# Head 0's zero fills moved, two heads' loads gated later, and extra TensorE work at head ends, in a 32-head attention kernel

## The chip, the cores and the metric

The kernel runs on one core of a Trainium2 chip. A core has five engines that run side by side, each through its own list of instructions in order: TensorE (PE, matrix multiply, results to the memory PSUM), VectorE (DVE), ScalarE (ACT, exponentials), GpSimd (POOL) and SyncE (SP, which here does nothing but issue DMAs). They wait for each other through semaphores. The metric is the device time of the core in microseconds (us). The kernel before has a median of 642.9 us of 3 runs (640.63 to 644.48).

## The reference

```
eps = 1e-6                                  # q, k, v: 1 x 32 heads x 2048 x 20, t: 32, all bf16
qn = q / (jnp.sqrt((q * q).sum(axis=-1, keepdims=True)) + eps)
kn = k / (jnp.sqrt((k * k).sum(axis=-1, keepdims=True)) + eps)
logits = jnp.einsum('bhqd,bhkd->bhqk', qn, kn) * t[None, :, None, None]
attn = _softmax(logits, axis=-1)
return jnp.einsum('bhqk,bhkd->bhqd', attn, v)
```

It is attention with normed queries and keys and one factor t per head. The product of a query and a key is 20 long, so a head's work is not in the matrix products but in 2048 x 2048 exponentials, 134 million in all.

## The kernel before

**The flow of a head.** k and q of a head are loaded to `qk_sb` in five DMAs (one for k, four for q: `add_loads`, line 585), v in one to `vaug`. DVE squares and sums them (lines 650, 654), takes the inverse root by a few small steps (`rs_u` line 658 to `rs_r`), and norms (line 696). SP then issues a DMA transposition of the normed head to `qkT` (line 707), and, when that has landed, ten copies by DMA, the "rotations": four from `qkT` to `qz` and six to `kR` (lines 708 to 716). They lay queries and keys out so that TensorE can run a QK product, whose contraction is only 20 long and padded to 32 rows, in three ways: as "32 rows" (up to four products beside each other in the array), as "64 rows" or as "128 rows", with the moving operand taken from `qz`, whose other rows are zero. The result is the same; what differs is how much of the array works. For head 0 the way is shorter: TensorE transposes, six DVE copies turn the keys (`kx`, line 768, the last of them is `rot0`), and three DMA transpositions bring them to `kR`.

**Two ways to the exponential.** A head's keys make 16 row tiles. `DVE_TILES[h]` of them go to DVE, the rest to ACT. On ACT's side, units of 512 columns are put in waves of 2 and 3 PSUM banks in turn (`psA`, two slots); TensorE fills a wave (`qk_mm`, line 790), ACT takes one exponential over it (line 891) to `p_ring`. On DVE's side (`psD`, two banks), DVE turns the logits into 16-bit integers that, read as half floats, are an exponential in the rough (line 950, one instruction for two banks, or for one where the tile is in `SPLIT`), and three shifted copies of them (line 960 on DVE, or line 964 on POOL, in pieces that fit beside DVE's work) are added up with scaled v (`vph`) so that the errors cancel. The PV products (line 810) of both ways, four matmuls a group, one for each 32-column strip of the array, add up in one PSUM bank, `psO`. When a head's last PV group is in, DVE transposes `psO` (line 823); only then may the next head's first PV group write it. The transposed sums are divided and stored (lines 832, 840).

**The order of the work** is not written by hand. Each instruction is a `Task` with an estimated duration, dependencies and a priority, and `list_schedule` (line 114) plays the engines through in time: each engine takes, when it is free, the ready task that its rules prefer. A DMA task occupies SP for `dur` and lands `lat` later. What comes out is the order of each engine's list; the chip then runs the lists in order, each instruction behind its semaphore waits. So the estimates, the numbers in `KNOBS` and `STAGES` (one choice of rules for every 10 us of planned time) and the priorities set the order, and nothing else. A QK task has `modes`: the planner keeps a sum of the array work that TensorE did in the last `TICK` = 3.41 us and takes the wider form (mode 1) as long as that sum stays under `LOAD`.

**SP's list** holds all loads (but one), transpositions, rotations and stores. A load of head h (from head 3 on) waits for an earlier head's transposition, its gate: head 3 for head 0's, head 4 for head 1's, later heads for that of head h - 4 (line 588, "LGATE" is 0). The priorities put a transposition and rotations of a head before loads that are due later, but only among tasks that are ready; a load that is ready while a transposition is still on its way is issued first.

**Before the first head**, DVE and POOL fill buffers with zeros and ones. `qz[0]` is filled by DVE, `qz[1]` and `qz[2]` by four POOL memsets each (line 561): those of `qz[1]` as soon as POOL gets to them, those of `qz[2]` after `rot0`.

## Time and profile before

| what | us |
| --- | --- |
| median of 3 runs | 642.9 (640.63 to 644.48) |
| the profiled execution, its own time | 645.58 |
| span of the profiled execution, first to last instruction | 643.8 |
| mean granted TensorE clock, of full speed | 0.987 |
| first exponential of ACT starts | 9.26 |
| last exponential ends | 638.66 |

All durations below are from the profiled execution; the time around its span is 1.8 us. An engine's busy time counts instructions in execution. Matmuls are pipelined: a group of four shows 0.40 us from start to end, eight show 0.61. A line of the chain of waits names an engine and a line of the kernel; "SPq" is SP's queue, that is time in which DMAs were being issued. The granted clock is the share of full speed at which TensorE ran in that stretch. Line 511 is the helper of most fills, line 508 that of all plain DMAs, so those are told apart by what they write.

### The profile page before, as it was taken

The page shows a single profiled execution, that of the slowest core. Times are in us where ns is not written, and L with a number is a line of the kernel's source. Part 1 is how long each engine was busy: PE and PEld are TensorE (multiplying, and loading weights), DVE is VectorE, ACT ScalarE, POOL GpSimd, SP SyncE. Part 2 cuts the span into 40 slices and gives each one's busy share as a digit, 9 for nine tenths or more (in the row PEclk, how much of TensorE's full clock was granted, in tenths as well). Part 3 has the DMA queues.
Part 4 walks back from the last instruction along what each step waited for, and adds up shares of the span by engine and source line. Part 5 has one row for each costly group of instructions (what it writes and reads, how often), then busy time and mean ns, then how long its engine had stood idle before and what let it go on. Part 6 is the DMA issues. An engine that isn't in the chain of part 4 may idle for free.

```text
span 643.8 us, 15022 instructions
## 1 busy us (share of the span) xinstructions
PE 593.1 (92%) x6127; PEld 171.4 (27%) x6143; DVE 627.0 (97%) x920; ACT 626.9 (97%) x558; POOL 428.0 (66%) x460
## 2 busy tenths in 40 slices
PE   7887998799999989999999899999999999999997
PEld 2221222222222222222222222222222222222222
DVE  8997999999999999999999999999999999999997
ACT  6997999999999999999999999999999999999996
POOL 4154677468787776767777586776877377665653
PEclk9997999999999989999999899999999999999999
DMA  4554445244344414344243333333343242322000
GB/s 59 68 72 82 72 69 77 44 67 59 59 65 73 65 29 68 52 73 65 51 68 48 54 61 59 69 52 51 58 73 56 36 72 37 66 50 56 5 3 16
DMA packets 196916, 36.39 MB, mean 57 GB/s; under 512 B 172656, under 2 KB 196848, under 8 KB 196848
## 3 DMA queue, kind: packets, MB, share of 16 engines
q1 hardware_dynamic: 196656, 35.32, 34.5%
q8 instruction: 48, 0.79, 0.5%
q14 instruction: 20, 0.16, 0.1%
q10 hardware_dynamic: 192, 0.11, 0.1%
HBM read 7.87 MB, written 2.62 MB: 16 GB/s over the span
## 4 chain that ended last, share of the span: by engine, by line
ACT 61%; DVE 28%; PE 6%; SPq 2%; issue 2%; DMA 1%; DVEq 0%
ACT p_ring L891 61%; DVE xt L950 17%; DVE ss L960 5%; PE psO L810 2%; SPq L508 2%; PE psA L790 2%; PE psD L790 1%; DVE rs_sum L654 1%; DVE oT L823 1%; DVE qkn L696 1%; DVE sq L650 1%; DMA kR<-qkT 0%; DVE o_stage L840 0%; DVE rs_u L658 0%; DMA qz<-qkT 0%
## 5 line engine op out<-in xcount | busy, mean ns | idle before, releaser
L891 ACT ACTIVATE p_ring<-psA 128x1024 bf16<-128x1024 f32 (+1 forms) x551 | 623.3, 1451 | 6.8 <-PE psA L790 5.8
L964 POOL INT64_ADD ss<-xt x430 | 420.8, 982 | 201.6 <-DVE xt L950 67.8
L950 DVE TENSOR_SCALAR xt<-psD 128x1024 int16<-128x1024 f32 (+1 forms) x410 | 414.0, 1025 | 9.3 <-PE psD L790 7.8
L810 PE MATMUL psO<-ss,vph 128*32 128x512 f16 x2016 | 172.9, 387 | 0.0
L960 DVE TENSOR_SCALAR ss<-xt 128x2048 int16<-128x2048 int16 x178 | 121.5, 685 | 0.5
L790 PE MATMUL psA<-qkT,kR 32*128 32x512 bf16 x636 | 110.2, 388 | 11.3 <-ACT p_ring L891 10.8
L810 PE MATMUL psO<-p_ring,vaug 128*32 128x512 bf16 x1376 | 119.2, 388 | 0.0
L790 PE MATMUL psA<-qz,kR 64*128 64x512 bf16 (+1 forms) x389 | 100.7, 391 | 9.3 <-ACT p_ring L891 8.6
L790 PE MATMUL psD<-qz,kR 64*128 64x512 bf16 (+1 forms) x313 | 84.8, 389 | 3.9 <-DVE xt L950 2.6
L790 PE MATMUL psA<-qkT 32*128 32x512 bf16 x196 | 62.4, 386 | 4.7 <-ACT p_ring L891 4.3
L810 PE MATMUL psO<-xt,vaug 128*32 128x512 f16 x672 | 66.7, 387 | 0.0
L810 PEld LDWEIGHTS psO<-ss,vph 128*32 128x32 f16 x2016 | 44.4, 94 | 76.7 <-issue 65.1
L790 PE MATMUL psA<-qz,qkT 64*128 64x512 bf16 (+1 forms) x145 | 50.4, 390 | 4.6 <-ACT p_ring L891 4.4
L790 PE MATMUL psD<-qkT,kR 32*128 32x512 bf16 x186 | 48.9, 384 | 3.1 <-DVE xt L950 2.5
L790 PEld LDWEIGHTS psA<-qkT,kR 32*128 32x128 bf16 x636 | 26.5, 91 | 77.2 <-ACT p_ring L891 73.8
L810 PEld LDWEIGHTS psO<-p_ring,vaug 128*32 128x32 bf16 x1376 | 31.3, 94 | 57.4 <-issue 49.7
L790 PEld LDWEIGHTS psA<-qz,kR 64*128 64x128 bf16 (+1 forms) x396 | 24.2, 93 | 71.9 <-ACT p_ring L891 68.6
L790 PE MATMUL psD<-qz,qkT 64*128 64x512 bf16 (+1 forms) x102 | 38.8, 388 | 2.4 <-DMA qz<-qkT 1.3
L790 PEld LDWEIGHTS psD<-qz,kR 64*128 64x128 bf16 (+1 forms) x318 | 20.9, 93 | 46.0 <-DVE xt L950 40.0
L790 PE MATMUL psD<-qkT 32*128 32x512 bf16 x65 | 24.4, 386 | 4.9 <-DMA kR<-qkT 2.9
L810 PEld LDWEIGHTS psO<-xt,vaug 128*32 128x32 bf16 x672 | 17.5, 94 | 30.5 <-issue 24.7
L696 DVE TENSOR_TENSOR qkn<-qk_sb,rs_r 128x640 bf16<-128x640 bf16 x31 | 25.3, 816 | 0.0
(58 smaller groups left out, 199.5 us busy)
## 6 DMA issues: line engine op xcount, KB each, us to landing
kR<-qkT SPq DMA_DIRECT2D x62, 96.0 KB, 2.1
qz<-qkT SPq DMA_DIRECT2D x127, 32.0 KB, 1.8
kR<-qkT SPq DMA_DIRECT2D x62, 64.0 KB, 2.0
qk_sb<-in_k_dram SPq DMA_DIRECT2D x32, 80.0 KB, 2.8
vaug<-in_v_dram SPq DMA_DIRECT2D x32, 80.0 KB, 3.2
qk_sb<-in_q_dram SPq DMA_DIRECT2D x124, 20.0 KB, 2.5
out_dram<-o_stage SPq DMA_DIRECT2D x31, 80.0 KB, 1.8
kR<-qkT SPq DMA_DIRECT2D x62, 32.0 KB, 1.9
```

Of the source, the lines that this page charges most:

```text
L508: return add(eng, name, lambda e, tk: e.dma_start(dst, src), dur, deps, pri, lat=lat, dma=key)
L650: c = [dv("sq", lambda e, tk, x=x, y=src: e.tensor_tensor(y, x, x, ALU.mult), 0.065 + 0.3335 * m, [u for k in range(m) for u in lds[h + k] ...
L654: sums.append(dv("sum", lambda e, tk, i=i, k=k, src=src: e.tensor_reduce(rs["sum"][:, 2 * R * (i + k):2 * R * (i + k + 1)], src[:, 2 * R * ...
L696: norm[h] = [dv("norm", lambda e, tk, x=x, b=b, i=i: e.tensor_tensor(qkn[b][:, :, 0:D], x[:, :, :], bc(rs["r"][:, 2 * R * i:2 * R * (i + 1 ...
L790: return eng.matmul(dst, lhsT, mov, tile_position=(p0, 0))
L810: last = eng.matmul(psO[32 * g:32 * g + 32, :], w, rhs_of(g), start=start, stop=False, skip_group_check=True, tile_position=(0, 32 * g))
L823: trO[h] = add("DVE", f"tr{h}", lambda e, tk: e.transpose(oT_all[:, so, :, :].rearrange("p r d -> p (r d)"), psO[:, :]), 0.63, [lambda: pv ...
L891: act[w] = add("ACT", f"exp{w}", lambda e, tk: e.activation(p_ring[:, p0 * 512:p0 * 512 + n], psA[:, slot * WAVES[0] * 512:slot * WAVES[0] ...
L950: u = add("DVE", f"t1.{j}.{k0}", lambda e, tk, o=o, c=c, w=512 * m: e.tensor_scalar(xt[sx][:, o:o + w], psD[:, c:c + w], X_MUL, X_ADD, ALU ...
L960: f = add("DVE", f"s{i}.{js[0]}", lambda e, tk, i=i, dst=dst: e.tensor_scalar(dst[:, be:be + w], xt[0][:, bx:bx + w], float(PHASES[i]), No ...
L964: f.alt = lambda c, n, i=i, dst=dst: lambda e, tk: e.int64_add(dst[:, be + 2 * c:be + 2 * (c + n)].bitcast(I64), xt[0][:, bx + 2 * c:bx + ...
```

## The change

It has five parts.

1. The POOL fills of `qz[1]` wait for `rot0` too, as those of `qz[2]` did. A new small buffer `nil` is filled with zeros by POOL.
2. The gates of the loads come from a table for heads 3 to 6: head 3 waits for head 0's transposition, 4 for 1's, 5 for 2's, 6 for 3's; from head 7 on it stays head h - 4. Before, head 5 waited for 1's and head 6 for 2's. The planner's estimates for loads of k, q and v change.
3. A new rule, `fill`: where TensorE has nothing ready, the PV sum of the current head is still open, the next QK task is at least 0.15 us away and the work in the last 3.41 us is under 3700, it is given a group of four matmuls of `nil` (zero weights) with `ones`, added to `psO`.
4. While the sum is closed (the head's PV groups are all in, and the next head's have not begun), the choice between QK forms counts only the work that will still be within the 3.41 us 1.2 us later, and so takes the wide form more often, if ACT or DVE has time for it. Elsewhere `LOAD` falls from 3550 to 3400.
5. `STAGES` has other numbers, `SPLIT` loses tile 82 and gains 124 and 157, and `DVE_TILES` moves tiles: head 3 has 7 instead of 6, head 8 5 instead of 6, head 27 7 instead of 6, head 31 6 instead of 7.

```diff
-    LOAD = 3550.0
+    LOAD = 3400.0
...
+    FILL = 3700.0
+    AHEADL = 1.2
+    FGAP = 0.15
...
+        left = collections.Counter(t.head for t in self.tasks if t.head is not None)
+        bank = [None]
+        self.fillers = []
+
+        def fill(now):
+
+            if not self.filler or bank[0] is None or not left[bank[0]] or now < self.LIGHT:
+                return
+            then = min(list(soon["PE"].values()) + [now + 0.6])
+            if then - now < self.FGAP:
+                return
+            while recent and recent[0][0] < now - self.TICK:
+                recent.popleft()
+            if sum(w for e, w in recent if e > then - self.TICK) >= self.FILL:
+                return
+            t = self.filler()
...
+                if e == "PE" and free[e] <= now + 1e-9 and not ready[e]:
+                    fill(now)
...
-                    load = sum(w for _, w in recent)
-                    if load + t.work < self.LOAD:
+                    shut = bank[0] is not None and not left[bank[0]]
+                    load = sum(w for x, w in recent if not shut or x > now + self.AHEADL - self.TICK)
+                    slack = (free["ACT"] if t.name[2] == "A" else free["DVE"] + sum(r[2].dur for r in ready["DVE"])) - now - t.modes[1][2] - 0.5
+                    if load + t.work < self.LOAD and (not shut or slack > 0 or sum(w for _, w in recent) + t.work < self.LOAD):
...
+        nil = sbuf("nil", [128, 32], BF16)
...
+        z_nil = memset("POOL", nil[:, :], 0.0, 0.1, -71)
...
-                             [lambda: rot0] if i > 1 else [], -70 + i) for g in range(NG)])
+                             [lambda: rot0], -70 + i) for g in range(NG)])
...
-            war = (norm[h - NB] if h >= NB else []) + ([lambda: [trn[max(h - 3, 0) if h < 5 + LGATE else h - 4]]] if h >= EARLY else [lambda: q0] if h == 2 else [])
+            war = (norm[h - NB] if h >= NB else []) + ([lambda: [trn[{3: 0, 4: 1, 5: 2, 6: 3}.get(h, h - 4)]]] if h >= EARLY else [lambda: q0] if h == 2 else [])
...
-                          war, pri - 0.01 if h else -50, f"k{b}", lat=4.5 if h else 2.2, dur=0.5)]
+                          war, pri - 0.01 if h else -50, f"k{b}", lat=4.2 if h else 2.2, dur=0.7 if h else 0.5)]
...
-                    lds[h].append(dma("SP", f"ldq{h}", dst, src, war, pri, f"q{b}", lat=4.5, dur=0.68))
+                    lds[h].append(dma("SP", f"ldq{h}", dst, src, war, pri, f"q{b}", lat=4.2, dur=0.9))
...
-                          war, pri + VPRI, f"v{bv}", lat=2.6, dur=1.4)
+                          war, pri + VPRI, f"v{bv}", lat=3.3, dur=0.7)
...
+        def null_mm(eng):
+            last = None
+            for g in range(NG):
+                last = eng.matmul(psO[32 * g:32 * g + 32, :], nil[:, :], ones[:, :], start=False, stop=False,
+                                  skip_group_check=True, tile_position=(0, 32 * g))
+            return last
```

## The prediction

> **What bounds the kernel now.** I read the page's busy times first, then its chain of work that ended last.

> ```profile
> span 643.8 us, 15022 instructions
> PE 593.1 (92%) x6127; PEld 171.4 (27%) x6143; DVE 627.0 (97%) x920; ACT 626.9 (97%) x558; POOL 428.0 (66%) x460
> ...
> ACT 61%; DVE 28%; PE 6%; SPq 2%; issue 2%; DMA 1%; DVEq 0%
> ...
> L891 ACT ACTIVATE p_ring<-psA 128x1024 bf16<-128x1024 f32 (+1 forms) x551 | 623.3, 1451 | 6.8 <-PE psA L790 5.8
> ...
> L950 DVE TENSOR_SCALAR xt<-psD 128x1024 int16<-128x1024 f32 (+1 forms) x410 | 414.0, 1025 | 9.3 <-PE psD L790 7.8
> ```

> ScalarE (ACT) and VectorE (DVE) are both 97% busy and share the chain. ACT's 551 exponentials take 623.3 us and stay: DVE_TILES still sums to 168, so (512 - 168) x 4 = 1376 units in alternating waves of 2 and 3 again make 551. Only ACT's idle time can go: 6.8 us before exponentials, of which 0.74 is before the first one at 9.26, and the time ahead of that one. After ACT's last exponential (618.32 + 20.34 = 638.66) 5.1 us of tail follow. DVE's idle time for psD (7.8 us) is of the same size, so both must gain together.

> Second, the busy times by stage (columns: PE, PEld, DVE, ACT, POOL with instruction counts, granted clock, DMA share, GB/s) show where the idle time sits.

> ```profile
> 16.00:32.00 16.00, 13.12 (x141) 3.50 (x131) 15.06 (x32) 15.20 (x15) 2.79 (x2) 1.00 0.56 66
> ...
> 48.00:64.00 16.00, 11.96 (x93) 2.69 (x90) 12.03 (x20) 12.74 (x12) 7.02 (x8) 0.79 0.48 82
> 64.00:80.00 16.00, 14.39 (x138) 3.93 (x136) 15.24 (x19) 15.78 (x15) 10.51 (x11) 0.92 0.49 73
> ...
> 224.00:240.00 16.00, 14.22 (x128) 3.67 (x127) 15.52 (x19) 15.39 (x15) 10.98 (x12) 0.89 0.21 29
> ...
> 352.00:368.00 16.00, 14.31 (x136) 3.92 (x135) 14.55 (x24) 14.90 (x15) 9.04 (x10) 0.89 0.37 60
> ```

> ACT loses 0.80, 3.26, 0.22, 0.61 and 1.10 us there; nearly every other stage after 32 us shows ACT at 16.00. In the last four the clock is below 1.

> Third, the chain in order of time through the 48 us hole (start, length, what), and the timeline of the start.

> ```profile
> 39.72 0.39 SPq L707
> 40.15 0.57 SPq L508
> ...
> 43.46 0.63 SPq L508
> ...
> 47.94 2.98 DMA kR<-qkT
> 50.97 0.61 PE psD L790 x2
> ```

> ```profile
> 4.00 1.95 POOL L561 MEMSET qz<- 128x512 bf16 x4
> 4.34 1.63 DVE L658 TENSOR_SCALAR rs_u<-rs_sum 128x32 int32<-128x32 int32 x1
> ```

> The SP queue, not a transfer's size, sets the hole: head 2's transposition is issued at 38.74, then head 5's five loads (40.15 to 43.41), and only at 43.46 head 2's ten rotations. The last, issued at 47.94, lands at 50.92; a psD matmul heads TensorE's (PE) queue and waits for it, and the psA matmuls are behind it.

> **1. Zero fills, first part: -1.4.** rs_u takes 1.63 us; its three other instances of that shape take 0.168 to 0.176. It ends at 5.97, 0.02 after the four qz fills that ran beside it. Without them 1.46 goes, and what is next on DVE (6.01 to 8.55) leads without a free step to the first exponential. PE's warm-up matmuls run to 6.13 and would hold the first transposition (7.29, now 5.83) for 0.3 us, but the path goes through the q transpositions at 7.70, now 6.24. The new fill of nil, a POOL memset like the 0.1 us ones, ends before 4.34. I take 1.4.

> **Fills, second part: +0.2, on DVE.** All eight now follow head 0's rotations, which end near 9.8 - 1.4 = 8.4; at 0.49 each they last to about 12.4. Nothing waits soon: head 1's qz rotations are issued at 26.85, POOL's next work starts at 22.69. On DVE, the fills at 9.89 to 11.93 left the two xt tiles beside them at 1.23 and 1.21 (median 1.22), but three vph scalings took 0.55 where two take 0.29 elsewhere, some 0.16 too long. The bounds are 0 and one more rs_u case, 1.46; I take 0.2, by the nearer row.

> [...]

> **2. Head 1's wait: -0.5.** At 28.7 to 30.7 the same thing stands in small: transposition at 21.01, landed 3.1 later (median), head 3's five loads from 23.23 to 26.75, and head 1's rotations behind them. Head 3's gate doesn't change. But the planner's cost of its loads goes from 0.5 + 4 x 0.68 = 3.2 to 0.7 + 4 x 0.9 = 4.3 us (here 3.5; at 16.31 four took 3.98), so it should fit one fewer ahead of the rotations, 0.6 to 0.9 us. Bounds 0 and 0.8 (ACT's loss).

> **3. Head 2's hole: -2.6.** In the new table heads 3 and 4 keep their gates; head 5 waits for head 2's transposition instead of head 1's, head 6 for head 3's. Head 6's loads are issued at 63.66, after head 3's transposition landed (50.61 + 3.1), so only head 5's move. Then the rotations can start at 38.74 + 3.1 = 41.84 instead of 43.46, the last is issued at 46.3 and lands after 2.0 (median) to 2.98: at 48.3 to 49.3. PE ran dry at 48.12, DVE at 48.91, ACT at 49.60; from matmul to exponential took 1.07 at half clock. So ACT keeps 0 to 0.6 of its 3.05 (2.44, and 0.61 at 54.6 from the slow clock behind the hole). Bounds 1.0 and 3.05. Behind the gated loads: everything later in SP's queue, head 3's transposition (50.61) first. Its rotations are issued by 61.6; head 3's matmuls come about a head (19.7) after 48, near 68, so 3.3 us more are covered. Head 5's squares run at 73.39, 33 us after its loads now.

> **4. Clock at head ends: -1.3.** Around 77, 234 and 357 the clock falls to 0.50 for 3 to 4 us. ACT then loses 0.29, 0.61 and 1.10 = 2.0, DVE 0.76, 0.48 and 1.45 = 2.7 (same table). In the 3 us before (231 to 234, 354 to 357) PE is busy 1.95 and 1.73. But 258 to 261 has 1.92 and keeps its clock: low activity is needed, not enough, so other executions lose other head ends. Four zero-weight matmuls per gap raise it wherever the head's sum is still open. Bounds 0 and 2.0; 1.3, since the closed stretch before each transposition of psO gets only wider QK matmuls.

> [...]

> **5. What they cost: +0.5.** A group of four fills the array for 0.21 (eight psO matmuls take 0.61, four 0.40). PE has some 106 gaps of 0.15 us or more after 9 us, without the two waits for rotations. A group starts only if the next QK is 0.15 away, so it delays that by up to 0.22 + 0.10 - 0.15 = 0.17. A two-bank wave has 0.60 to spare (225.75 + 0.39 against 226.74), a three-bank one 0.14 (224.88 + 0.39 against 225.41). If a sixth hit the latter at 0.03 each, that is 0.5. Bounds 0 and 106 x 0.17 = 18.

> **6. Retuning: 0.** One more split tile costs DVE two pairs at 1.29 instead of two tiles at 1.13, some 0.3. The last head's DVE tile less saves three psO groups, up to 0.6, of PE's 1.25 us of backlog after 638.90; I take 0.2 to 0.3. LOAD 3550 to 3400 narrows some QK matmuls in mid-head: 0 to two more clock losses (0.3 to 1.1 each), taken as 0. The STAGES numbers only reorder.

> **Sum.** -1.4 + 0.2 - 0.5 - 2.6 - 1.3 + 0.5 = -5.1. The profiled execution took 645.58 (span 643.8 and 1.8 around), so its successor takes 640.5; ACT's floor (7.8 + 623.3 + 5.1 + 1.8 = 638.0) is not crossed. That execution is 2.7 above the median, 642.9, of runs that spread from 640.63 to 644.48. Taking 2.7 off gives 637.8; as part of it may be clock losses that the median run doesn't have to give back, I add 0.4: **638.2 us**.

> **Rivals and chances.** Within 0.5% (3.2 us) a measurement can't tell a change from none.
> - Forecast: 0.55.
> - The wait only moves (0.18): loads or another transposition take head 5's place before a rotation, or head 4's loads (33.83 to 38.69), which stood before head 2's transposition though its input was ready at 36.63, stay there. For it: SP issues without pause from 10.5 to 52. Against: ten issues fit before 48. Terms 2 and 3 go: 641.3.
> - The change doesn't hold the clock (0.09): zero weights don't count, or the closed stretch decides. For it: no row has such a matmul. Against: warm-up with ones keeps 1.00. Term 4 goes: 638.2 + 0.9 = 639.1. [...]
> - All idle time goes (0.08): 638.0 - 2.7 = 635.3.
> - Slower (0.10): fills on PE delay the three-bank waves. The place is the 0.14 us of spare time; from 0.05 us per gap (5.2 / 106) the gain is gone, at 0.1 it is 637.7 + 10.6 = 648.3. Against: the groups of psO matmuls already run in that place, and ACT is at 16.00.

> Range: 635.2 to 642.4, which leaves out the slower rival and the ends of the others. Faster by over 0.5% (under 639.7): forecast nearly whole, the floor, most of the clock case, a bit of the moved wait: 0.70. Slower: 0.10. The rest 0.20.

> **What would show it.** rs_u at 0.17 and the first exponential near 7.8 (1); no DVE instruction stretched at 8 to 12.5 (fills); head 2's rotations right behind its transposition's landing and ACT without idle time at 48 (2, 3); clock 1.00 in every slice (4); ACT's idle time before exponentials under 3 us (5). The prediction is wrong if ACT shows many idle times of 0.05 to 0.2 behind psA matmuls, or a DMA is again what a psD matmul waits for.

## The result, and the profile after

The changed kernel has a median of 638.58 us (636.86 to 639.09, 8 runs) against 643.69 (640.63 to 645.88, 8 runs) for the kernel before. The ratio is 0.9917, with a 95% interval of 0.9894 to 0.994: 5.1 us faster. Its profiled execution took 638.55 (span 636.8). One run of the experiments, the fourth of b3 with 834.35, ran at a mean granted clock of 0.557 and stands in no ratio.

The page after, in the lines that answer to those of before:

```profile
span 636.8 us, 15281 instructions
...
PE 596.2 (94%) x6267; PEld 170.9 (27%) x6267; DVE 627.2 (99%) x926; ACT 626.0 (98%) x558; POOL 423.4 (66%) x461
...
ACT 88%; DVE 7%; PE 5%; issue 0%
...
L938 ACT ACTIVATE p_ring<-psA 128x1024 bf16<-128x1024 f32 (+1 forms) x551 | 622.5, 1429 | 2.3 <-PE psA L837 2.3
...
L998 DVE TENSOR_SCALAR xt<-psD 128x1024 int16<-128x1024 f32 (+1 forms) x412 | 414.0, 1021 | 2.4 <-PE psD L837 1.8
```

The work is the same, and the chain is now nearly ACT alone: its idle time before exponentials went from 6.8 to 2.3, DVE's before psD's readers from 9.3 to 2.4. SPq, 2% of the chain before, is gone from it. The stages that had lost time (columns as before: PE, PEld, DVE, ACT, POOL, clock, DMA share, GB/s):

```profile
16.00:32.00 16.00, 13.80 (x143) 3.78 (x143) 15.86 (x34) 15.94 (x15) 3.82 (x4) 1.00 0.51 75
...
48.00:64.00 16.00, 12.90 (x136) 3.54 (x134) 14.36 (x24) 14.49 (x13) 7.92 (x7) 1.00 0.43 71
64.00:80.00 16.00, 13.71 (x135) 3.71 (x128) 15.97 (x27) 16.00 (x16) 10.02 (x10) 1.00 0.50 76
...
224.00:240.00 16.00, 14.35 (x150) 3.85 (x142) 15.97 (x22) 16.00 (x15) 12.96 (x17) 1.00 0.18 46
```

Every clock is 1.00. One loss is left, 1.51 us at 61 us. The timelines of the start and of SP and PE round that loss:

```profile
4.38 0.18 DVE L697 TENSOR_SCALAR rs_u<-rs_sum 128x32 int32<-128x32 int32 x1
...
7.96 4.62 ACT L938 ACTIVATE p_ring<-psA 128x1024 bf16<-128x1024 f32 x4 [0.74 <-PE psA L837]
8.54 3.90 POOL L600 MEMSET qz<- 128x512 bf16 x8 [4.40 <-DVE kx L815]
...
31.33 2.92 SPq L746 DMA_TRANSPOSE qkT<-qkn  x1
34.29 0.57 SPq L546 DMA_DIRECT2D qk_sb<-in_k_dram  x1
...
36.94 2.54 SPq L546 DMA_DIRECT2D qz<-qkT  x4
...
44.69 1.79 SPq L546 DMA_DIRECT2D qk_sb<-in_k_dram  x1
...
47.85 1.36 SPq L746 DMA_TRANSPOSE qkT<-qkn  x1
...
54.26 3.77 SPq L546 DMA_DIRECT2D kR<-qkT  x6
...
61.63 0.39 PE L837 MATMUL psD<-qz,kR 64*128 64x512 bf16 x2 [1.51 <-DVE ss L1008]
```

rs_u takes 0.18 instead of 1.63. Head 2's transposition is now issued ahead of head 4's loads (at 31.33 instead of 38.74, the loads from 34.29), and its rotations follow from 36.94 instead of 43.46. The loss at 61 is the old hole one head later and half as long: head 5's loads now stand about head 3's transposition, and of head 3's six kR copies the last, issued at 57.45, landed 4.1 us later (median 2.0), at 61.54. DVE is named as releaser of the psD matmul at 61.63, but it had been done for 0.96.

From profile to profile the span fell by 7.0: 1.3 before the first exponential, 0.7 at 28 us, 1.75 between 48 and 64, 2.0 at the three head ends where the clock had fallen, 0.8 in the exponentials' own time (which lies between 622.5 and 625.0 in the profiles of the experiments too), and 0.4 after the last one. The median fell by less, since the profiled execution of before was one of its slower ones.

### The profile page after: what moved, and what is told of

The parts are those of the page before. It is cut to its first block, busy times and chain, and to the rows that moved or that the text cites. A ratio compares the mean times of both kernels' runs of the same rounds, so it can differ in the third digit from the quotient of the medians.

```text
span 636.8 us, 15281 instructions
## 1 busy us (share of the span) xinstructions
PE 596.2 (94%) x6267; PEld 170.9 (27%) x6267; DVE 627.2 (99%) x926; ACT 626.0 (98%) x558; POOL 423.4 (66%) x461
## 4 chain that ended last, share of the span: by engine, by line
ACT 88%; DVE 7%; PE 5%; issue 0%
ACT p_ring L938 88%; DVE xt L998 3%; PE psO L857 2%; DVE ss L1008 1%; PE psA L837 1%; PE psO L760 1%; PE psD L837 1%; DVE rs_sum L693 0%; DVE oT L870 0%; PE psO L802 0%; DVE sq L689 0%; DVE qkn L735 0%; DVE o_stage L887 0%; DVE vph L652 0%; DVE ones L549 0%
## 5 line engine op out<-in xcount | busy, mean ns | idle before, releaser
L938 ACT ACTIVATE p_ring<-psA 128x1024 bf16<-128x1024 f32 (+1 forms) x551 | 622.5, 1429 | 2.3 <-PE psA L837 2.3
L1012 POOL INT64_ADD ss<-xt x430 | 416.1, 972 | 200.3 <-DVE xt L998 51.9
L998 DVE TENSOR_SCALAR xt<-psD 128x1024 int16<-128x1024 f32 (+1 forms) x412 | 414.0, 1021 | 2.4 <-PE psD L837 1.8
L857 PE MATMUL psO<-ss,vph 128*32 128x512 f16 x2016 | 175.6, 385 | 0.0
L1008 DVE TENSOR_SCALAR ss<-xt 128x2048 int16<-128x2048 int16 x182 | 124.9, 688 | 0.6
L837 PE MATMUL psD<-qz,kR 64*128 64x512 bf16 (+1 forms) x359 | 97.7, 384 | 7.1 <-DVE xt L998 4.9
L837 PE MATMUL psA<-qkT 32*128 32x512 bf16 x220 | 67.1, 384 | 4.6 <-ACT p_ring L938 4.3
L837 PE MATMUL psD<-qz,qkT 64*128 64x512 bf16 (+1 forms) x123 | 46.5, 384 | 2.0 <-DVE xt L998 1.8
L837 PE MATMUL psA<-qz,qkT 64*128 64x512 bf16 (+1 forms) x124 | 43.2, 385 | 0.6 <-ACT p_ring L938 0.4
L837 PE MATMUL psD<-qkT,kR 32*128 32x512 bf16 x145 | 37.7, 382 | 3.2 <-DVE xt L998 2.3
L837 PEld LDWEIGHTS psD<-qz,kR 64*128 64x128 bf16 (+1 forms) x359 | 23.9, 93 | 57.9 <-DVE xt L998 50.4
L693 DVE TENSOR_REDUCE rs_sum<-sq 128x32 f32<-128x640 bf16 x31 | 25.1, 810 | 0.0
```

The costliest lines, as they stand in the source:

```text
L693: sums.append(dv("sum", lambda e, tk, i=i, k=k, src=src: e.tensor_reduce(rs["sum"][:, 2 * R * (i + k):2 * R * (i + k + 1)], src[:, 2 * R * ...
L837: return eng.matmul(dst, lhsT, mov, tile_position=(p0, 0))
L857: last = eng.matmul(psO[32 * g:32 * g + 32, :], w, rhs_of(g), start=start, stop=False, skip_group_check=True, tile_position=(0, 32 * g))
L938: act[w] = add("ACT", f"exp{w}", lambda e, tk: e.activation(p_ring[:, p0 * 512:p0 * 512 + n], psA[:, slot * WAVES[0] * 512:slot * WAVES[0] ...
L998: u = add("DVE", f"t1.{j}.{k0}", lambda e, tk, o=o, c=c, w=512 * m: e.tensor_scalar(xt[sx][:, o:o + w], psD[:, c:c + w], X_MUL, X_ADD, ALU ...
L1008: f = add("DVE", f"s{i}.{js[0]}", lambda e, tk, i=i, dst=dst: e.tensor_scalar(dst[:, be:be + w], xt[0][:, bx:bx + w], float(PHASES[i]), No ...
```

## Experiments

Twelve kernels. The "a" ones start from the changed kernel, the "b" ones from the kernel before. In a1, a2, a5, a9, a10, b1, b6 and b8 the lists of the engines are those of the starting kernel but for the edit named; in a4, a6, b2 and b3 the planner writes new lists. Each ratio is to runs of the kernel before on the same chip.

**a1, the fills early again.**

```diff
-                             [lambda: rot0], -70 + i) for g in range(NG)])
+                             [lambda: rot0] if i > 1 else [], -70 + i) for g in range(NG)])
```

> The changed kernel with one part undone: the four POOL fills of the second qz buffer run early again, as before; the order of every engine's list is the same as in the changed kernel. Theory (the fills hold back rs_u): rs_u takes 1.6 us again instead of 0.18, the first exponential starts near 9.3 instead of 7.96, and the whole is 1.3 to 1.4 us longer than the changed kernel (near 640). Rival (the start is set by something beside it, such as the loads): the first exponential stays near 8 and the time near 638.6.

Measured: 640.42 (12 runs), ratio 0.9952 (0.9925 to 0.998). rs_u takes 1.69, the first exponential starts at 9.29. The median is 1.8 us above the changed kernel's, 2.3 by the two ratios. The theory holds by the trace; in time the two intervals overlap.

**b1, the fills alone.** The same edit, the other way, in the kernel before.

> The kernel before with one part of the change done alone: the fills of the second qz buffer wait for head 0's rotations too; the order of every engine's list is that of the kernel before. Theory: rs_u at 0.17 to 0.18, first exponential near 7.9, and 1.3 to 1.4 us less than the kernel before (ratio 0.998). Rival (the time given back at the start is lost again at the waits for head 1's and head 2's rotations, whose DMAs hang on other things): first exponential near 7.9, but ScalarE's idle time before exponentials grows from 6.8 by as much, and the time does not change.

Measured: 642.74 (12 runs) against 644.07, ratio 0.9974 (0.9944 to 1.0003). rs_u takes 0.18, the first exponential starts at 8.24. ACT's idle time falls too, from 6.8 to 5.9, so nothing is lost again behind it. The 1.3 us are the size expected, though the interval just reaches no change.

**a2, the zero-weight groups taken out of the list.** (There are 31 groups, 124 matmuls; the expectation's 35 was too many.)

```diff
+        order["PE"] = [t for t in order["PE"] if t.name != "pvnil"]
+        self.fillers = []
```

> The changed kernel with the 35 groups of zero-weight matmuls left out of TensorE's list after planning, so that everything else stands in the same order; the result is the same, since they add zeros. Theory (these groups keep the clock up at head ends): some head ends show a granted clock near 0.5 again for 3 to 4 us, each costing ScalarE 0.3 to 1.1 us: 0 to 2 us more, near 639.5. Rival 1 (zero weights do nothing for the clock, the planner's other choices do): clock 1.00 and no change. Rival 2 (the groups delay QK matmuls): faster than the changed kernel by some 0.5 us.

Measured: 643.72 (12 runs), ratio 0.9985 (0.9958 to 1.0012). That is 5.1 us above the changed kernel by the medians, 4.4 by the two ratios, whose intervals lie apart: without these groups nothing measurable is left of the gain. The stages of a2, where the changed kernel's run shows ACT at 16.00 and the clock at 1.00:

```profile
64.00:80.00 16.00, 13.14 (x106) 3.25 (x103) 15.60 (x27) 15.07 (x14) 10.02 (x10) 0.86 0.52 78
80.00:96.00 16.00, 16.00 (x173) 4.72 (x173) 14.56 (x19) 15.12 (x14) 11.40 (x11) 0.93 0.50 79
224.00:240.00 16.00, 14.12 (x113) 3.29 (x109) 15.27 (x20) 14.96 (x15) 12.55 (x16) 0.79 0.15 35
368.00:384.00 16.00, 13.69 (x118) 3.35 (x119) 13.70 (x16) 14.30 (x14) 10.06 (x9) 0.79 0.40 66
```

ACT's idle time before exponentials is 6.3 instead of 2.3. The mean clock of a2's runs is 0.973 to 0.981, that of the changed kernel's 0.994 to 1.000. The mechanism is as forecast, the size is more than twice the forecast's upper bound of 2.

**a5, every zero-weight group twice.**

```diff
-            for g in range(NG):
+            for g in [x for _ in range(2) for x in range(NG)]:
                 last = eng.matmul(psO[32 * g:32 * g + 32, :], nil[:, :], ones[:, :], start=False, stop=False,
```

> The changed kernel with every group of zero-weight matmuls issued twice (70 groups instead of 35, eight matmuls in a row), the order otherwise the same. Theory (a group delays a three-bank wave by a few hundredths at most, as it stands where nothing is ready): each doubled group adds 0.21 us of array time in gaps that hold about one, so 35 x 0 to 0.1 = 0 to 3 us more, and ScalarE's idle time before exponentials grows from 2.3 by as much. Rival (they run in true idle time and cost nothing): no change within 0.5 us.

Measured: 639.06 (11 runs), ratio 0.9921 (0.9895 to 0.9946), 0.5 above the changed kernel, inside both intervals. In the profiled run ACT's idle time is 1.8, not more. Another 31 groups cost 0 to 0.5 us, so the first 31 probably cost about as little.

**a9, the wide QK forms put back.** The new rule had made 23 QK tasks wide while a sum is closed.

```diff
                         self.use(t, 1)
+                        if shut:
+                            wides.append(t)
...
+        for t in wides:
+            keep = t.dur
+            self.use(t, 0)
+            t.dur = keep
```

> The changed kernel with the 23 QK tasks that the new rule made wide while a head's sum is closed put back to their narrow form after planning; order, zero-weight groups and all else stay. Theory (wide forms there hold the clock like the zero-weight groups do elsewhere): clock near 0.5 again behind two to five head ends, 0.3 to 1.1 us each, so 1 to 4 us more. Rival (23 tasks are too little work to matter): clock 1.00 and no change within 0.5 us.

Measured: 638.33 (6 runs), ratio 0.9916 (0.9894 to 0.9938), clock 1.0 in the profiled run. The theory falls: this part of the change does nothing that can be measured here.

**b2, the gates alone, and b3, the estimates alone.**

```diff
-            ... [lambda: [trn[max(h - 3, 0) if h < 5 + LGATE else h - 4]]] ...
+            ... [lambda: [trn[{3: 0, 4: 1, 5: 2, 6: 3}.get(h, h - 4)]]] ...
```

> The kernel before with the new table of gates alone; the planner's estimates of the loads stay. Theory as predicted (the gate of head 5's loads makes the hole at 48 us): head 5's loads leave their place ahead of head 2's rotations, ScalarE's idle time there falls from 3.05 to under 0.6 us, the time by 2.5 us. Rival (the estimates set the place of the loads): the hole stays over 2 us.

> The kernel before with the new estimates of the loads (k 0.7, q 0.9, v 0.7 us) alone, gates as before; the planner writes the same lists for all engines whether the gates are old or new. Rival of the prediction (the estimates and not the gates remove the hole): one q load fewer stands ahead of head 1's and head 2's rotations, ScalarE's idle time at 29 and 48 us falls from 3.85 to under 1, the time by about 3 us unless the other head ends, planned anew with old choices, lose more. Theory as predicted (the gate does it): the hole stays over 2 us.

Measured: b2 656.19 (4 runs), ratio 1.0203 (1.0164 to 1.0243); b3 657.72 to 663.0 (3 runs), ratio 1.0236 (1.019 to 1.0282). Both remove the hole: ACT is busy for 8.00 of 8 us between 48 and 56 in either. So gates and estimates each do it. In the changed kernel the gates do nothing: with the old ones and the new estimates the planner writes the same lists. But both kernels are slower by 12 us and more, where 2.5 to 3 us less was expected. The reason is on the page; b3's busy times and DVE's shifted copies:

```profile
PE 597.8 (90%) x6122; PEld 168.1 (25%) x6143; DVE 645.3 (98%) x952; ACT 628.5 (95%) x558; POOL 383.4 (58%) x427
...
L960 DVE TENSOR_SCALAR ss<-xt 128x2048 int16<-128x2048 int16 x210 | 142.8, 686 | 1.5
```

POOL is busy for 383.4 us instead of 428.0, and DVE makes 210 shifted copies instead of 178. DVE is 18 us busier (645.3 against 627.0) and ends last. The likely reason is that the numbers in STAGES were searched for another plan and let POOL take fewer copies in this one; no run changed them alone.

**a4, the old estimates in the changed kernel, and a6, head 5 gated one head later still.**

```diff
-                          ... lat=4.2 if h else 2.2, dur=0.7 if h else 0.5)]
+                          ... lat=4.5 if h else 2.2, dur=0.5)]
...
-                    ... lat=4.2, dur=0.9))
+                    ... lat=4.5, dur=0.68))
...
-                          ... lat=3.3, dur=0.7)
+                          ... lat=2.6, dur=1.4)
```

> The changed kernel with the old estimates of the loads, the new gates kept. If the gates remove the hole, no wait for rotations over 1 us before 60 us, and a time within 1 us of the changed kernel's. If the estimates do, a wait of 1.5 to 3 us is back at head 1's or head 2's rotations, and the time is 2 to 4 us longer (640.5 to 642.5).

a6's edit is `5: 3` for `5: 2` in the table of gates.

> The changed kernel with head 5's loads gated by head 3's transposition, not head 2's. The changed kernel still loses 1.5 us on ScalarE at 60 to 62 us, after head 3's rotations. Theory (head 5's loads of 44.7 to 50.6 us now delay head 3's transposition and rotations by 1 to 2 us: the wait has moved by one head): that idle time falls under 0.5 us and the time by about 1 us. Rival (the last rotation lands late, 4.1 us after its issue, because of what else is in flight, the v load above all): the idle time stays over 1 us.

Measured: a4 654.72 (4 runs), ratio 1.0167 (1.0145 to 1.0189); a6 653.06 (4 runs), ratio 1.0139 (1.0121 to 1.0156). The waits behaved: a4 shows no wait for rotations before 60 us (ACT idle 0.23 in all from 48 to 56), and a6 has no idle time at 61. Both expectations of the time failed, and again through DVE:

```profile
PE 597.3 (92%) x6282; PEld 172.4 (26%) x6303; DVE 640.8 (98%) x947; ACT 626.6 (96%) x558; POOL 393.3 (60%) x438
```

This is a6: 203 shifted copies on DVE instead of the changed kernel's 182. ACT is done near 636, DVE goes on to 649.

**b6, head 5's loads moved in SP's list, and nothing else.**

```diff
...
+            move(("ldk5", "ldq5"), "rot2")
```

The new `move` puts them behind head 2's last rotation.

> The kernel before with one thing changed after planning: in SP's list head 5's five loads stand behind head 2's ten rotations instead of ahead of them. All other lists are those of the kernel before. Theory (SP's order makes the hole at 48 us, whatever puts it so): head 2's rotations start 1.6 us earlier, the last lands at 48.3 to 49.3, ScalarE's idle time there falls from 3.05 to under 0.6, and the time by 2.5 us (ratio 0.996). Rival (the transfers, not their place, are late): the hole stays over 2 us.

Measured: 644.21 (12 runs), ratio 1.0001 (0.9981 to 1.0021). The hole is gone: the psD matmul that had waited until 50.97 starts at 48.07, and ACT loses 0.25 between 48 and 56 instead of 3.12. But the time is the same: the interval leaves room for 1.2 us at most, not for the 2.5 expected. In its profiled run the next head end loses more than that of before (stages of b6; the kernel before had ACT at 7.78 and 7.93, the clock at 0.84 and 0.95):

```profile
72.00:80.00 8.00, 6.53 (x32) 1.27 (x33) 7.46 (x13) 6.87 (x6) 4.31 (x6) 0.57 0.40 64
80.00:88.00 8.00, 7.96 (x75) 1.99 (x77) 7.10 (x13) 7.32 (x7) 4.42 (x5) 0.79 0.58 77
```

That is 1.8 us there against 0.3. ACT's idle time before exponentials falls only from 6.8 to 5.4. What else the hole's removal should give doesn't show in runs that differ by their clocks (0.978 to 0.995).

**b8, three parts without a new plan:** the fills, b6's move, and 28 zero-weight groups put where the plan of before leaves TensorE a gap inside an open sum (`then - now`).

```diff
...
+                while then - now >= 0.15:
...
+                    if sum(x for _, x in work) >= 4300.0:
+                        break
+                    f = self.filler()
```

> The kernel before with three things done without planning anew: the fills of the second qz buffer wait for head 0's rotations, head 5's loads stand behind head 2's rotations in SP's list, and 28 groups of zero-weight matmuls stand where the plan leaves TensorE a gap of 0.15 us or more inside an open sum. No retuned numbers, no changed forms of QK. Theory (the three parts carry the whole gain): -1.4 - 2.5 - 0 to 1.5, that is 638.5 to 640, level with the changed kernel. Rival (the new plan itself carries a good part): 641 or more.

Measured: 641.75 (12 runs), ratio 0.9958 (0.9938 to 0.9979). The rival holds: some 3 us of the gain (3.2 by the medians, 2.6 by the ratios, whose intervals just touch) need the new plan. The profiled run still shows the clock at 0.79 to 0.80 in four stretches of 8 us (72, 216, 256 and 352). Its runs follow their clock: 638.63 at 0.997, 643.89 at 0.989.

**a10, the changed kernel with head 5's loads behind head 3's rotations in SP's list.**

```diff
...
+            move(("ldk5", "ldq5"), "rot3")
```

> The changed kernel with head 5's five loads behind head 3's ten rotations in SP's list, all other lists the same. The changed kernel's profiled run lost 1.51 us on ScalarE at 61 us. Theory (head 5's loads at 44.7 to 50.5 hold up head 3's transposition and rotations): no idle time over 0.2 us there, and 0.5 to 1.5 us less than the changed kernel (near 637.5). Rival (a single late landing, 4.1 us instead of 2.0, that comes and goes): no change in the median.

Measured: 637.35 (6 runs, 636.85 to 639.2), ratio 0.9907 (0.9885 to 0.9929). The idle time at 61 is gone (ACT 8.00 of 8 from 56 to 64). The median is 1.2 below the changed kernel's, the best of all here, but the intervals overlap, so it is not shown to be faster. Its profiled run (638.73) loses 0.78 one head later instead, from 72 to 80, at a clock of 0.79.

## Why the prediction was right, and where its steps were not

The time (638.58 for 638.2) and the sum (-5.1 for -5.1 by medians) came out, and so did the two main mechanisms: the hole at 48 goes and the clock holds. That the sum fits to a tenth is luck, since errors in its terms cancelled.

- **Step 1, -1.4: right** (rs_u has five other instances of its shape, not three, all of 0.17 to 0.18). -1.30 to the first exponential in the changed kernel, 1.3 and 1.8 us by b1 and a1. The second part of it, +0.2 on DVE, was small but real: three vph scalings took 0.55 again, and one shifted copy at 11.89 took 1.09 instead of 0.69 beside the fills.
- **Steps 2 and 3, -0.5 and -2.6: the waits right, the agent and the worth not.** The losses fell by 0.7 and 1.75 in the profiles. The step said that the gate moves the loads; in the changed kernel the new estimates do that with or without the gate. It also kept head 4's loads ahead of head 2's transposition; they went behind it, and the rotations start 4.9 us before the 41.84 of the step. And it counted the idle time at its full price: b6 took away 2.9 us of idle time and gained nothing measurable. The rival "the wait only moves" was half right: 1.5 us came back one head later, where a psD matmul waits for a DMA again, one of the prediction's own signs of being wrong.
- **Step 4, -1.3: the right mechanism, mis-sized.** It took 1.3 of the 2.0 that ACT lost at three head ends of one profile. From profile to profile the whole 2.0 went, and in a2 the groups are worth 4.4 to 5.1, since the new plan without them loses more clock (0.978) than the old one (0.989). The rival "the change doesn't hold the clock" is refuted: zero weights count.
- What a lost share of the clock costs is less sure. In 65 runs of the kernel before, each with its mean clock, a straight line by least squares falls by 3.5 us for each 0.01 of clock and reaches 640.3 at 1.00; the one run at 1.000 took 641.09. At the median clock, 0.989, that would be 3.8 us. But such a line can't tell the cost of a low clock from that of the delays that bring it about, and of the 17.1 us that the profile before shows at half clock up to the tail, 6.8 lie behind the hole of step 3. In the 37 runs of the changed kernel, a5, a9 and a2, which differ by their zero-weight groups and QK forms alone, the line falls by 2.3 for each 0.01: 2.6 at 0.989.
- Not every fall follows a long gap of PE: in the 6 us before, the longest is 0.62 for the fall at 234.39 in the kernel before, and 0.74 for the one at 372.34 in a2.
- What sets 258 to 261 apart can be read from the traces. In each of the 14 profiles, the clock changes only at whole multiples of 3.41 us from its first change (in the kernel before it falls to 0.50 at 50.07, 77.38, 234.39 and 357.27, which lie 8, 46 and 36 times 3.413 us apart, and stays there for 6.83 us after the first of them and 3.41 after the others). On that grid, count each matmul as 0.21 us (from the 0.40 us of four and 0.61 of eight) times the share of the array's rows and columns that it uses, from 10 to 630 us. Then the array was filled to 0.36 or less in 28 of the 31 stretches that a fall follows, and in only 15 of the 2472 behind which the clock stays at 1.00. In the kernel before, the falls come after 0.25, 0.39, 0.33 and 0.27; the stretch from 258.28 has 0.47. In the changed kernel the lowest is 0.41; without its zero-weight groups six stretches would have 0.30 to 0.36.
- **Step 4's closed stretch** was the reason for taking 1.3 and not 2.0. a9 shows that it needed no care.
- **Step 5, +0.5: the right size** (a5: 0 to 0.5). The slower rival, groups that delay three-bank waves, did not come about.
- **Step 6, 0: wrong in kind.** "The STAGES numbers only reorder" failed. They also decide how many shifted copies POOL takes from DVE: the planner, run by itself, leaves 201 of them on DVE instead of 182 when the changed kernel has the old numbers, and 213 instead of 178 when the kernel before has the new ones. On the chip these numbers were not tried alone. But four kernels whose plan was changed without searching them anew had 203 to 210 copies on DVE and were slower than their start by 12 to 16 us. So the retuning is probably what kept the new plan from costing that; in the sum it stood as nothing because both sides of it were left out.

What stays open: whether b6's larger loss at the next head end follows from the earlier start or is chance, and how much of b8's missing 3 us is the placing of the groups rather than the rest of the plan. What made the landing at 61 late stays open too. In a10 and a6 the same copy landed after 2.1 us, but there both head 5's loads and the v load that followed the copy stand elsewhere. And with SP's list as in the changed kernel it landed after 3.8, 3.0, 2.1 and 2.1 in a9, a1, a5 and a2: it comes and goes.

## What to carry to other kernels

Where a clock depends on activity, price it by a kernel that differs in that activity alone, over many runs, as a2 does. The idle time in one profile prices one plan and one execution, and a line through the runs of one kernel mixes the clock's cost with that of what lowers it. A planner's tuned numbers belong to one plan; test a part of a change with the instruction lists held fixed, or its effect drowns in what the numbers do to a new plan. And idle time taken from one place is worth its length only if the places behind it have no losses waiting.
